# Attention and two MoE layers on one core: the first MoE's tokens in chunks of 512, 256, 256 and 512, the second MoE's w_out converted at its use, and two buffers of transposed probabilities

## The chip, the cores and the metric

The kernel runs on one core of one Trainium2 chip. The metric is device time in microseconds (us) from one launch, and the median of several runs is compared. The engines are named as the profile names them: PE is TensorE (PEld its weight loads), DVE is VectorE, ACT is ScalarE, POOL is GpSimd, and SP is the engine whose queue issues all of this kernel's DMAs.

## The reference

```python
# q, k, v: 2 x 8 heads x 768 x 64; window 128, 4 sink columns
scores = np.where(is_sink | in_window, scale * (q @ k.T), -1e9)
a = softmax(scores)
x = (a @ v).transpose(0, 2, 1, 3).reshape(1536, 512)
...
h = x @ w1_in                                   # 512 -> 2048
g = np.where(h >= 1, h, np.where(h <= -1, 0.0, (h + 1) ** 2 / 4))
x = g @ w1_out                                  # 2048 -> 512
...
h = x @ w2_in
g = h * np.clip(h + 3.0, 0.0, 6.0) / 6.0
out = g @ w2_out
```

The weights are 64-bit floats, q, k and v 32-bit ones.

## The kernel before

**The MoE layers.** Tokens (1536) lie along the free dimension, features along the 128 partitions. Each layer is worked through in chunks of N = 512 tokens, three in each layer: chunks 0, 1 and 2 are the first MoE's, chunks 3, 4 and 5 the second's. A chunk has 16 steps, one for each 128 of the 2048 hidden features. A step is an `h_group` (12 matmuls into one of the two banks of `ps_h`) and, LAG = 2 steps later, the `y_group` of the same features (12 matmuls into the four accumulator banks `ps_y`). Every operand is kept as a high and a low part in float32r (`xh`/`xl`, `wih`/`wil`, `gh`/`gl`, the two halves of `wo`), and every product is three matmuls. Between `h_group` and `y_group`, ACT and DVE apply the activation and split the result into `gh` and `gl`: five operations in the first MoE, four in the second.

**The weights.** A 64-bit weight tile (`raw`, 512 KB, four buffers) is loaded, turned into a float32 tile `w` by ACT, DVE and POOL (`narrow`), and split into a high and a low part: `take`. A tile of w_in stays in SBUF until its layer is over. A tile of w_out is used by one step of each chunk: its two parts are written to HBM (`wo_d`) and read back (`load_wo`) by later chunks. `queue` says at which step each tile is taken. The second MoE's w_out is taken in steps 16 to 31, that is during chunk 1, into tiles of its own called `early`, and its w_in during chunk 2.

**The attention.** The 48 units of work (128 queries of two heads each) stand in four groups: group 0 is done ahead of chunk 0 (the prologue), and the others are spread over the slots of the steps (four slots in a step). While chunk c runs, the attention of chunk c + 1's tokens is done. For a unit PE first computes two scores (`ps_s`, one bank for each head), DVE adds the mask and takes the maximum (L326), ACT exponentiates (L345), DVE normalises (L337 to L340). Three units later PE transposes the probabilities (`turn`: `ps_t`; `sinks`: `ps_k`), ACT copies them out of PSUM into `pt` and `pts` (L364), and one unit after the last transpose of a pair of heads `mix` multiplies them with v (`ps_v`), and the result goes into the next chunk's `xh` and `xl`. There is one `pt` buffer, so that the first copy of the next pair waits for the mix of this pair. Once the first `y_group` has begun, scores, transposes and mixes share two PSUM banks (pool `ps_a`).

**What sets the order.** PE and SP run in the order in which the code is written. The order of DVE, ACT and POOL is laid out ahead by a scheduler with a timeline of its own. [...]

**Outputs of a chunk** are written to HBM (`x2_d`) at the chunk's end and read back as the second MoE's input (`load_x`, at step 4 of the chunk before).

Of the kernel before, what the change touches and what calls it, by code (L numbers as in the profile page):

```python
# [16 lines left out]
P = 128  # L17
# [4 lines left out]
F64_HIGH = 122879.984375  # L22


N = 512

GROUPS = [(0, 0, 0, 4), (1, 0, 4, 2), (1, 1, 0, 2), (2, 1, 2, 4)]

DIST = 3
MIX_LAG = 1  # L30
# [39 lines left out]
def f32(ap):  # L70
    return ap.bitcast(F32)
# [3 lines left out]
def sink_attention_moe_moe_kernel(  # L75
# [20 lines left out]
    FC = w1_in.shape[0]  # L96
    SCALE = 1.0 / float(D) ** 0.5
    fast = fast_case(S, n_sink, window)
    NCH = NT // N
    chunks = [(m, c * N) for m in range(2) for c in range(NCH)]  # L100

    consts = ctx.enter_context(tc.tile_pool(name="consts", bufs=1))
    wpool = ctx.enter_context(tc.tile_pool(name="w", bufs=1))
# [7 lines left out]
    ps_a = ctx.enter_context(tc.tile_pool(name="ps_a", bufs=2, space=bass.MemoryType.PSUM))  # L111


    x2_d = [[dram.tile([DM, N], F32R, name=f"x2{part}{c}_d") for part in "hl"] for c in range(NCH)]
    wo_d = [[dram.tile([P, 2 * DM], F32R, name=f"wo{m}_{fc}_d") for fc in range(FC)] for m in range(2)]


# [33 lines left out]
    xparts = {}  # L151

    def x_tile(ci, part, dtype, name):
        return x_p.tile([P, KC, N], dtype, tag=f"{part}{ci % 2}", name=f"{name}{ci}", bufs=1)
# [41 lines left out]
    def take(m, which, fc):  # L196

        t = raw.pop((m, which, fc))
        if which == "i":
            hi = wpool.tile([P, DM], F32R, tag=f"wih{fc}", name=f"wih{m}_{fc}")  # L200
            lo = wpool.tile([P, DM], F32R, tag=f"wil{fc}", name=f"wil{m}_{fc}")
            wi[m, fc] = (hi.rearrange("p (k f) -> p k f", f=P), lo.rearrange("p (k f) -> p k f", f=P))
        else:
            w = wo_tile(m, fc) if m == 0 else wo_p.tile([P, 2, DM], F32R, tag="early", name="early", bufs=2)
            hi, lo = w[:, 0, :], w[:, 1, :]

        def split(src):
# [38 lines left out]
    def build_fast_attention(at_p):  # L246
# [121 lines left out]
        def turn(j, u):  # L368
            b, i0, nq, first, nb = geom(pairs[j][0])
            i = i0 + u  # L370
            if u == 0:
                pt[j] = (
                    at_p.tile([P, 2, NQ, 2, P], F32, tag="pt", name="pt", bufs=1),
                    at_p.tile([NS, 2, NQ, P], F32, tag="pts", name="pts", bufs=1),
                )
            p = probs[j, u]
            w = widths[min(i, 2)]
            ps = bank("ps_t").rearrange("p (e n q) -> p e n q", e=2, n=2)
            lo = 1 if i == 0 else 0
# [138 lines left out]
    gparts, ytiles = {}, {}  # L518

    def load_x(ci):  # L520
        m, t0 = chunks[ci]
        for part, t in zip((0, 1), x_tiles(ci)):
            nc.sync.dma_start(out=f32(t), in_=f32(x2_d[ci - NCH][part]).rearrange("(k p) n -> p k n", p=P))

    def load_x1(ci):
        xh, xl = x_tiles(ci)
        src = x1_d[0]
        for kc in range(KC):
            t = g_p.tile([P, N], F32, tag="r", name="xraw")
            nc.sync.dma_start(out=t, in_=src[kc * P:(kc + 1) * P, chunks[ci][1]:chunks[ci][1] + N])  # L530
            high(xh[:, kc, :], t, N)
            low(xl[:, kc, :], t, xh[:, kc, :], N)
# [95 lines left out]
    with tc.manual_schedule(engines={mybir.EngineType.PE, mybir.EngineType.SP}):  # L628
        nc.vector.memset(half, 0.5)
        make_identity(nc, ident)  # L630
        with ExitStack() as att:
# [17 lines left out]
            for s in range(len(seq) + LAG):  # L649
# [71 lines left out]
```

## Time and profile before

| | us |
|---|---|
| median of 3 runs | 715.59 (714.6 to 723.47) |
| profiled execution, own time | 720.04 |
| its span, first to last instruction | 718.2 |
| PE busy, share of the span | 670.4, 93% |
| DVE busy | 418.7, 58% |
| ACT busy | 329.2, 46% |
| POOL busy | 98.2, 14% |

The profile was taken from one execution, whose own time is 1.8 us above its span and 4.45 us above the median. The busy shares are means over parts with different limits: the prologue runs from 0 to 69.2 us, chunk 0 to 225.1, chunk 1 to 360.7, and the other four chunks and the last two `y_group`s fill the rest.

### The profile page before, as it was taken

Reading aid. Unit: us, or ns where it says so; the run is one execution under the profiler, and the core shown is the slowest. Engines: PE = TensorE matmul, PEld = TensorE weight load, DVE = VectorE, ACT = ScalarE, POOL = GpSimd, SP = SyncE. Lnnn points to the kernel's source line nnn. Section 1 sums busy time; section 2 is a strip of 40 time slices with the busy share of each in tenths; the row PEclk is TensorE's granted clock in tenths of the full one; section 3 lists DMA queues with packets and bytes.
Section 4 is the critical chain, followed back from the end, with each engine's and each line's share of the span. In section 5 each row is a group of like instructions: output and inputs, shape, how many; then the busy total and the mean of one; then the engine's idle time right before and its main releaser. Section 6 shows DMA issues by size and latency. Waiting matters only on the chain.

```text
span 718.2 us, 8789 instructions
## 1 busy us (share of the span) xinstructions
PE 670.4 (93%) x3008; PEld 506.3 (70%) x3008; DVE 418.7 (58%) x916; ACT 329.2 (46%) x674; POOL 98.2 (14%) x83
## 2 busy tenths in 40 slices
PE   6888778988889999989999999999999999999997
PEld 3445555656557656667688888888888888888886
DVE  5989987779766777678377996322223222232222
ACT  6678856565554656366345563322222222222222
POOL 2212251313102021113001431000000000000000
PEclk9989988799989989999999999999999999999999
DMA  7144636365347668196539842472326432152221
GB/s 264 63 133 140 216 117 201 115 191 188 116 139 253 223 253 309 42 358 204 177 115 381 304 168 88 167 273 88 103 74 212 175 112 88 60 205 89 89 88 59
DMA packets 45869, 119.16 MB, mean 166 GB/s; under 512 B 4304, under 2 KB 13568, under 8 KB 45824
## 3 DMA queue, kind: packets, MB, share of 16 engines
q1 hardware_dynamic: 45824, 118.60, 47.8%
q8 instruction: 24, 0.39, 0.2%
q14 instruction: 21, 0.17, 0.1%
HBM read 92.36 MB, written 26.21 MB: 165 GB/s over the span
## 4 chain that ended last, share of the span: by engine, by line
PE 66%; DVE 16%; DMA 10%; ACT 4%; SPq 2%; issue 2%; POOL 0%; ACTq 0%; POOLq 0%
PE ps_y L586 30%; PE ps_h L542 29%; PE ps_v L419 5%; DMA raw1o<-moe_w_out_dram 3%; DMA raw0o<-moe_w_out_dram 3%; DVE p L340 2%; PE ps_s L319 2%; DMA raw0i<-moe_w_in_dram 2%; DVE w L190 2%; DVE p L326 2%; DVE w L188 2%; ACT w L185 1%; DVE ps_h L553 1%; DVE r L552 1%; DVE wil L149 1%
## 5 line engine op out<-in xcount | busy, mean ns | idle before, releaser
L586 PE MATMUL ps_y<-gh,wo 128*128 128x512 f32 x768 | 263.1, 400 | 1.7 <-DVE xl L149 1.7
L586 PEld LDWEIGHTS ps_y<-gh,wo 128*128 128x128 f32 x768 | 146.3, 190 | 35.9 <-issue 3.9
L542 PE MATMUL ps_h<-xh,wih 128*128 128x512 f32 x384 | 155.7, 405 | 2.1 <-ACT xh L142 1.6
L542 PE MATMUL ps_h<-xl,wih 128*128 128x512 f32 x384 | 151.5, 394 | 0.5 <-DVE xl L149 0.5
L586 PE MATMUL ps_y<-gl,wo 128*128 128x512 f32 x384 | 151.4, 394 | 0.0
L542 PE MATMUL ps_h<-xh,wil 128*128 128x512 f32 x384 | 151.4, 394 | 0.0
L149 DVE TENSOR_TENSOR gl<-ps_h,gh 128x512 fp32r<-128x512 f32 x96 | 66.1, 689 | 102.3 <-ACT gh L142 101.8
L142 ACT ACTIVATE gh<-ps_h 128x512 fp32r<-128x512 f32 x96 | 57.2, 596 | 134.7 <-PE ps_y L586 109.9
L556 DVE SCALAR_TENSOR_TENSOR ps_h<-r,ps_h 128x512 f32<-128x512 f32 x48 | 33.4, 696 | 103.8 <-ACT r L555 103.8
L542 PEld LDWEIGHTS ps_h<-xh,wih 128*128 128x128 f32 x384 | 72.9, 190 | 24.0 <-issue 7.1
L319 PE MATMUL ps_s<-kraw,qraw 64*128 64x260 f32 (+2 forms) x192 | 55.2, 471 | 32.9 <-DVE nm L326 26.1
L542 PEld LDWEIGHTS ps_h<-xh,wil 128*128 128x128 f32 x384 | 73.1, 190 | 15.6
L542 PEld LDWEIGHTS ps_h<-xl,wih 128*128 128x128 f32 x384 | 73.1, 190 | 14.6 <-DVE xl L149 0.8
L586 PEld LDWEIGHTS ps_y<-gl,wo 128*128 128x128 f32 x384 | 73.4, 191 | 13.9
L555 ACT ACTIVATE r<-ps_h,half 128x512 f32<-128x512 f32 x48 | 33.0, 688 | 104.1 <-PE ps_h L542 104.1
L319 PEld LDWEIGHTS ps_s<-kraw,qraw 64*128 64x128 f32 x192 | 26.6, 217 | 56.7 <-DVE nm L326 37.9
L345 ACT ACTIVATE p<-p,nm 128x260 f32<-128x260 f32 (+2 forms) x96 | 46.6, 486 | 33.0 <-DVE nm L326 32.5
L552 DVE SCALAR_TENSOR_TENSOR r<-r 128x512 f32<-128x512 f32 x48 | 39.8, 829 | 17.3 <-ACT r L551 17.3
L326 DVE CUSTOM_DVE_ANT_0 p<-ps_s,mask 128x260 f32<-128x260 f32 (+2 forms) x96 | 36.8, 396 | 13.9 <-PE ps_s L319 13.8
L188 DVE TENSOR_SCALAR w<-w 128x512 f32<-128x512 f32 x64 | 32.4, 506 | 20.8 <-ACT w L185 20.6
L340 DVE TENSOR_SCALAR p<-p,sm 128x260 f32<-128x260 f32 (+2 forms) x96 | 40.2, 458 | 0.7
L551 ACT ACTIVATE r<-ps_h,half 128x512 f32<-128x512 f32 x48 | 32.6, 680 | 16.4 <-PE ps_h L542 16.3
(62 smaller groups left out, 666.5 us busy)
## 6 DMA issues: line engine op xcount, KB each, us to landing
wo<-wo_d SPq DMA_DIRECT2D x80, 512.0 KB, 5.2
raw0i<-moe_w_in_dram SPq DMA_DIRECT2D x16, 512.0 KB, 5.6
raw0o<-moe_w_out_dram SPq DMA_DIRECT2D x16, 512.0 KB, 4.6
wo_d<-wo SPq DMA_DIRECT2D x16, 512.0 KB
raw1o<-moe_w_out_dram SPq DMA_DIRECT2D x16, 512.0 KB, 7.8
wo_d<-early SPq DMA_DIRECT2D x16, 512.0 KB, 4.9
raw1i<-moe_w_in_dram SPq DMA_DIRECT2D x16, 512.0 KB
x2h_d<-yh SPq DMA_DIRECT2D x12, 256.0 KB, 2.3
```

Source lines behind the costliest of these rows:

```text
L142: nc.scalar.activation(out=dst, in_=src, func=AF.Copy)
L149: nc.vector.tensor_tensor(out=dst, in0=src, in1=f32(hi), op=ALU.subtract)
L188: nc.vector.tensor_scalar(out=f32(c), in0=f32(c), scalar1=F64_LOW, scalar2=F64_HIGH, op0=ALU.max, op1=ALU.min)
L319: nc.tensor.matmul(banks[e], tq[rows, u * P:(u + 1) * P], tk[rows, c0:c0 + w], start=True, stop=True)
L326: nc.vector.tensor_tensor_reduce(out=p[:, e, :], in0=banks[e], in1=masks[min(i, 2)], scale=-SCALE, scalar=BIG, op0=ALU.add, op1=ALU.min, a ...
L340: nc.vector.tensor_scalar_mul(out=p[:, e, :], in0=p[:, e, :], scalar1=sm[:, e:e + 1])
L345: nc.scalar.activation(out=p[:, e, :], in_=p[:, e, :], func=AF.Exp, scale=-1.0, bias=nm[:, e:e + 1], accum_out=sm[:, e:e + 1],)
L419: nc.tensor.matmul(ps[e * D:(e + 1) * D, u0 * P:u1 * P], l, r, start=n == 0, stop=n == len(ops[0]) - 1)
L542: nc.tensor.matmul(ps, w[:, kc, :], x[:, kc, :], start=i == 0, stop=i == len(ops) - 1)
L552: nc.vector.scalar_tensor_tensor(out=r, in0=r, scalar=1.0, in1=r, op0=ALU.min, op1=ALU.mult)
L556: nc.vector.scalar_tensor_tensor(out=ps, in0=r, scalar=1.0, in1=ps, op0=ALU.min, op1=ALU.mult)
L586: nc.tensor.matmul(ys[dm], a[:, cs], b, start=fc == 0 and i == 0, stop=fc == FC - 1 and i == 2)
```

## The change

The first MoE has four chunks, of 512, 256, 256 and 512 tokens; the second keeps three of 512. So there are seven chunks, 0 to 3 and 4 to 6. Every tile keeps its size, and the 256-token chunks use half of it: their matmuls have 256 moving columns, and their ACT and DVE operations 256 elements. Group 1 of the attention belongs to chunk 1 and group 2 to chunk 2, so chunk 0 runs beside 8 units of attention instead of 16, chunk 1 beside the next 8, and chunk 2 (256 tokens) beside group 3, as chunk 1 (512 tokens) did before. The converted tiles of w_out are now read back in chunks 1, 2 and 3, and 5 and 6.

The second MoE's w_out is taken in steps 64 to 79, during chunk 4, straight into the tiles that chunk 4's `y_group`s read; the `early` tiles are gone. Its w_in is taken in steps 49 to 64, during chunk 3.

There are two buffers of `pt` and `pts`. The HBM copies of x2 are one tensor for all chunks instead of one for each.

```diff
+CHUNKS = [[512, 256, 256, 512], [512, 512, 512]]
-GROUPS = [(0, 0, 0, 4), (1, 0, 4, 2), (1, 1, 0, 2), (2, 1, 2, 4)]
+GROUPS = [(0, 0, 0, 4), (1, 0, 4, 2), (2, 1, 0, 2), (3, 1, 2, 4)]
...
-    NCH = NT // N
-    chunks = [(m, c * N) for m in range(2) for c in range(NCH)]
+    NCH = len(CHUNKS[0])
+    chunks = [(m, sum(CHUNKS[m][:c]), n) for m in range(2) for c, n in enumerate(CHUNKS[m])]
...
-            w = wo_tile(m, fc) if m == 0 else wo_p.tile([P, 2, DM], F32R, tag="early", name="early", bufs=2)
+            w = wo_tile(m, fc)
...
-                    at_p.tile([P, 2, NQ, 2, P], F32, tag="pt", name="pt", bufs=1),
-                    at_p.tile([NS, 2, NQ, P], F32, tag="pts", name="pts", bufs=1),
+                    at_p.tile([P, 2, NQ, 2, P], F32, tag="pt", name="pt", bufs=2),
+                    at_p.tile([NS, 2, NQ, P], F32, tag="pts", name="pts", bufs=2),
...
-        ps = ps_h.tile([P, N], F32, tag="h", name="ps_h")
+        ps = ps_h.tile([P, N], F32, tag="h", name="ps_h")[:, :n]
...
     for fc in range(FC):
-        queue.append((FC + fc, 1, "o", fc))
-    for fc in range(FC):
+        queue.append((NCH * FC + fc, 1, "o", fc))
         queue.append(((NCH - 1) * FC + 1 + fc, 1, "i", fc))
...
-                if 0 <= a < len(seq) and seq[a][0] not in (0,):
+                if 0 <= a < len(seq) and seq[a][0] not in (0, NCH):
                     load_wo(chunks[seq[a][0]][0], seq[a][1])
```

**PE in chunk 0, where a pair of heads follows another.** The row with ps_s is a unit's two scores, ps_v the mix of the earlier pair, and what stands in brackets is the engines whose semaphores a row waits for. Before, from the second half of a `y_group` to the mix:

```order
L319 MATMUL ps_s<-kraw,qraw 128x128 [waits DMAHW1_49,DMAHW0_49,DVE_49]
L319 MATMUL ps_s<-kraw,qraw 128x128 [waits DVE_49]
L586 MATMUL ps_y<-gh,wo_917 128x512
L586 MATMUL ps_y<-gl,wo_917 128x512
L586 MATMUL ps_y<-gh,wo_917 128x512 x2
L586 MATMUL ps_y<-gl,wo_917 128x512
L586 MATMUL ps_y<-gh,wo_917 128x512
L419 MATMUL ps_v<-pts,vs 64x256 [waits DMAHW6_49,DVE_49]
```

And in the changed kernel at the same unit, three steps later in the chunk (the mix stands half an `h_group` behind the last row):

```order
L321 MATMUL ps_s<-kraw,qraw 128x128 [waits DMAHW6_49,DMAHW5_49,DVE_49]
L321 MATMUL ps_s<-kraw,qraw 128x128 [waits Activation_49]
L589 MATMUL ps_y<-gh,wo_1138 128x512
L589 MATMUL ps_y<-gl,wo_1138 128x512
L589 MATMUL ps_y<-gh,wo_1138 128x512 x2
L589 MATMUL ps_y<-gl,wo_1138 128x512
L589 MATMUL ps_y<-gh,wo_1138 128x512
```

The second score waited for DVE, and waits now for ACT. Of the 27 units scored in chunk 0 and after, 10 had a second score that waits for DVE; in the changed kernel 1 has.

**DVE while group 3 of the attention is done.** `ps_h`, `r` and `gl` are the MoE's activation and split, `p`, `nm` and `sm` the attention, `raw1o`, `w` and `early` the conversion of the second MoE's w_out. Before, a step and a half of chunk 1:

```order
L149 TENSOR_TENSOR early<-w_2563,early 128x512
L149 TENSOR_TENSOR gl<-ps_h,gh 128x512
L188 TENSOR_SCALAR w_2787<-w_2787 128x512
L189 TENSOR_SCALAR raw1o_2548<-raw1o_2548 128x512
L326 ISA p,nm<-ps_s,mask_136 128x260
L326 ISA nm 128x1
L190 SCALAR_TENSOR_TENSOR w_2787<-w_2787,raw1o_2548 128x512
L552 SCALAR_TENSOR_TENSOR r<-r 128x512
L326 ISA p,nm<-ps_s,mask_136 128x260
L326 ISA nm 128x1
L149 TENSOR_TENSOR early<-w_2641,early 128x512
L553 TENSOR_TENSOR ps_h<-ps_h,r 128x512
```

And a step of chunk 2 of the changed kernel:

```order
L150 TENSOR_TENSOR gl<-ps_h,gh 128x256
L555 SCALAR_TENSOR_TENSOR r<-r 128x256
L339 TENSOR_SCALAR sm<-sm 128x2
L556 TENSOR_TENSOR ps_h<-ps_h,r 128x256
L340 RECIPROCAL sm<-sm 128x2
L342 TENSOR_SCALAR p<-p,sm 128x260 x2
L150 TENSOR_TENSOR gl<-ps_h,gh 128x256
L328 ISA p,nm<-ps_s,mask_132 128x260
L328 ISA nm 128x1
L328 ISA p,nm<-ps_s,mask_132 128x260
L328 ISA nm 128x1
```

No conversion stands between them any more, in chunk 1 and chunk 2 alike, and the MoE's rows have half the elements.

**DVE in chunk 4 of the changed kernel**, the second MoE's first, where before only the L556 and `gl` rows and four `yl` of the chunk before stood:

```order
L559 SCALAR_TENSOR_TENSOR ps_h<-r,ps_h 128x512
L190 TENSOR_SCALAR w_4843<-w_4843 128x512
L191 TENSOR_SCALAR raw1o_4694<-raw1o_4694 128x512
L192 SCALAR_TENSOR_TENSOR w_4843<-w_4843,raw1o_4694 128x512
L150 TENSOR_TENSOR gl<-ps_h,gh 128x512
L190 TENSOR_SCALAR w_4888<-w_4888 128x512
L191 TENSOR_SCALAR raw1o_4739<-raw1o_4739 128x512
L192 SCALAR_TENSOR_TENSOR w_4888<-w_4888,raw1o_4739 128x512
L559 SCALAR_TENSOR_TENSOR ps_h<-r,ps_h 128x512
L150 TENSOR_TENSOR wo_4842<-w_4843,wo_4842 128x512
```

The low part of w_out tile 7 is made behind the activation of step 6 of that chunk; the `y_group` that reads it is in step 9.

## Rows read from the trace of the kernel before

**Rows 1.** Busy time by stage: stretch, length, PE, PEld, DVE, ACT, POOL, clock, DMA.

```profile
0.00:69.20 69.20, 55.53 (x241) 30.53 (x241) 56.68 (x203) 49.22 (x136) 16.54 (x29) 0.93 0.46 147
69.20:225.10 155.90, 134.63 (x594) 92.89 (x593) 120.45 (x289) 90.65 (x199) 37.09 (x25) 0.90 0.51 166
225.10:360.70 135.60, 126.45 (x617) 90.16 (x617) 96.08 (x211) 75.58 (x157) 24.68 (x17) 0.97 0.62 225
360.70:447.70 87.00, 87.00 (x385) 72.09 (x384) 71.76 (x107) 45.69 (x77) 19.84 (x13) 1.00 0.60 218
447.70:534.80 87.10, 87.10 (x386) 72.12 (x386) 24.78 (x37) 22.85 (x36) 0.00 (x0) 1.00 0.41 145
```

**Rows 2.** The chain that ended last, in order of time: start, length, what.

```profile
298.81 2.91 PE ps_v L419 x24
...
371.75 2.72 PE ps_h L542 x12
```

**Rows 3.** What PE waited for in chunk 0: total us, times, longest.

```profile
PE ps_s L319 <- DVE nm L326: 14.3, 8, 3.8
```

**Rows 4.** What PE waited for in chunk 1.

```profile
PE ps_s L319 <- DVE nm L326: 2.6, 2, 1.5
```

**Rows 5.** Timeline around one such wait in chunk 0: start, length, engine.

```profile
97.60 0.48 PE L319 MATMUL ps_s<-kraw,qraw 64*128 64x128 f32 x2
...
101.57 0.28 DVE L326 CUSTOM_DVE_ANT_0 p<-ps_s,mask 128x128 f32<-128x128 f32 x1
...
101.91 0.79 PE L319 MATMUL ps_s<-kraw,qraw 64*128 64x128 f32 x2 [3.83 <-DVE nm L326]
```

**Rows 6.** Busy time in the stretch behind that wait, columns as Rows 1.

```profile
100.00:111.00 11.00, 9.09 (x30) 5.87 (x31) 7.67 (x20) 4.02 (x10) 4.52 (x3) 0.53 0.11 24
```

**Rows 7.** Two waits of ACT over the whole span.

```profile
ACT pt L364 <- PE ps_v L419: 19.4, 11, 5.8
...
ACT w L185 <- DMA raw1o<-moe_w_out_dram: 12.3, 6, 4.1
```

**Rows 8.** Busy time in parts of chunk 0, columns as Rows 1.

```profile
69.20:111.00 41.80, 33.47 (x152) 22.46 (x151) 36.55 (x90) 27.70 (x60) 14.27 (x9) 0.88 0.50 163
69.20:153.20 84.00, 70.25 (x313) 47.95 (x311) 70.10 (x164) 52.97 (x113) 25.72 (x17) 0.86 0.51 164
153.20:225.10 71.90, 64.37 (x284) 44.94 (x283) 50.36 (x126) 37.69 (x86) 11.37 (x9) 0.95 0.52 168
```

**Rows 9.** DVE's groups by shape over the whole span.

```profile
L340 DVE TENSOR_SCALAR p<-p,sm 128x260 f32<-128x260 f32 x64 | 26.9, 461 | 0.4
...
L326 DVE CUSTOM_DVE_ANT_0 p<-ps_s,mask 128x260 f32<-128x260 f32 x64 | 25.9, 420 | 5.5 <-PE ps_s L319 5.4
...
L337 DVE TENSOR_SCALAR sm<-sm 128x2 f32<-128x2 f32 x48 | 13.6, 287 | 5.6 <-ACT p L345 5.4
...
L149 DVE TENSOR_TENSOR xl<-ps_v,xh 128x512 fp32r<-128x512 f32 x8 | 5.5, 687 | 9.6 <-ACT xh L142 9.6
...
L149 DVE TENSOR_TENSOR xl<-ps_v,xh 128x256 fp32r<-128x256 f32 x8 | 3.3, 417 | 2.8 <-ACT xh L142 2.8
```

**Rows 10.** PE's timeline in chunk 0, transposes and a score.

```profile
74.67 0.27 PE L382 MATMUL ps_t<-ident,p 128*128 128x128 f32 x1
...
75.46 0.48 PE L542 MATMUL ps_h<-xh,wih 128*128 128x512 f32 x1
...
77.03 0.71 PE L319 MATMUL ps_s<-kraw,qraw 64*128 64x260 f32 x4
77.67 0.50 PE L542 MATMUL ps_h<-xh,wih 128*128 128x512 f32 x1
```

**Rows 11.** Weight loads at the same place.

```profile
75.44 0.19 PEld L542 LDWEIGHTS ps_h<-xh,wih 128*128 128x128 f32 x1
75.55 0.19 PEld L542 LDWEIGHTS ps_h<-xl,wih 128*128 128x128 f32 x1
```

**Rows 12.** Issues of the tiles of w_out that are read back: count, size, us to landing.

```profile
wo<-wo_d SPq DMA_DIRECT2D x80, 512.0 KB, 5.2
```

More of the change, by code (lines that the diff above doesn't have):

```diff
@@ L111, in sink_attention_moe_moe_kernel @@
     ps_a = ctx.enter_context(tc.tile_pool(name="ps_a", bufs=2, space=bass.MemoryType.PSUM))
-    x2_d = [[dram.tile([DM, N], F32R, name=f"x2{part}{c}_d") for part in "hl"] for c in range(NCH)]
+    x2_d = [dram.tile([DM, NT], F32R, name=f"x2{part}_d") for part in "hl"]
     wo_d = [[dram.tile([P, 2 * DM], F32R, name=f"wo{m}_{fc}_d") for fc in range(FC)] for m in range(2)]
@@ L153, in x_tile @@
     def x_tile(ci, part, dtype, name):
-        return x_p.tile([P, KC, N], dtype, tag=f"{part}{ci % 2}", name=f"{name}{ci}", bufs=1)
+        t = x_p.tile([P, KC, N], dtype, tag=f"{part}{ci % 2}", name=f"{name}{ci}", bufs=1)
+        return t[:, :, :chunks[ci][2]]
     def x_tiles(ci):
@@ L520, in load_x @@
     def load_x(ci):
-        m, t0 = chunks[ci]
-        for part, t in zip((0, 1), x_tiles(ci)):
-            nc.sync.dma_start(out=f32(t), in_=f32(x2_d[ci - NCH][part]).rearrange("(k p) n -> p k n", p=P))
+        m, t0, n = chunks[ci]
+        for part, t in zip(x2_d, x_tiles(ci)):
+            nc.sync.dma_start(out=f32(t), in_=f32(part).rearrange("(k p) n -> p k n", p=P)[:, :, t0:t0 + n])
     def load_x1(ci):
@@ L527, in load_x1 @@
         src = x1_d[0]
+        m, t0, n = chunks[ci]
         for kc in range(KC):
[L529 to L532, printed above, removed]
+            t = g_p.tile([P, N], F32, tag="r", name="xraw")[:, :n]
+            nc.sync.dma_start(out=t, in_=src[kc * P:(kc + 1) * P, t0:t0 + n])
+            high(xh[:, kc, :], t, n)
+            low(xl[:, kc, :], t, xh[:, kc, :], n)
     def h_group(s, slot):
         ci, fc = seq[s]
-        m, _ = chunks[ci]
+        m, _, n = chunks[ci]
         hi, lo = wi[m, fc]
         xh, xl = x_tiles(ci)
-        ps = ps_h.tile([P, N], F32, tag="h", name="ps_h")
+        ps = ps_h.tile([P, N], F32, tag="h", name="ps_h")[:, :n]
         ops = [(w, x, kc) for kc in range(KC) for w, x in ((hi, xh), (hi, xl), (lo, xh))]
@@ L544, in h_group @@
                 slot()
-        r = g_p.tile([P, N], F32, tag="r", name="r")
-        gh = g_p.tile([P, N], F32R, tag="gh", name="gh")
-        gl = g_p.tile([P, N], F32R, tag="gl", name="gl")
+        r = g_p.tile([P, N], F32, tag="r", name="r")[:, :n]
+        gh = g_p.tile([P, N], F32R, tag="gh", name="gh")[:, :n]
+        gl = g_p.tile([P, N], F32R, tag="gl", name="gl")[:, :n]
         with tc.high_priority(200):
@@ L556, in h_group @@
                 nc.vector.scalar_tensor_tensor(out=ps, in0=r, scalar=1.0, in1=ps, op0=ALU.min, op1=ALU.mult)
-        bal.tensor(len(ops) * N / 2.26)
-        bal.add("act", 260 + N / 1.2)
-        bal.add("dve", (2 - m) * (150 + N / 0.96))
+        bal.tensor(len(ops) * n / 2.26)
+        bal.add("act", 260 + n / 1.2)
+        bal.add("dve", (2 - m) * (150 + n / 0.96))
         def split():
             with tc.high_priority(200):
-                high(gh, ps, N, True)
-                low(gl, ps, gh, N)
+                high(gh, ps, n, True)
+                low(gl, ps, gh, n)
         defer(split)
@@ L571, in y_group @@
         ci, fc = seq[s]
-        m, t0 = chunks[ci]
+        m, t0, n = chunks[ci]
         w = wo.pop((m, fc))
@@ L577, in y_group @@
             spare.clear()
-            ytiles[ci] = [ps_y.tile([P, N], F32, tag=f"y{i}", name="ps_y") for i in range(KC)]
+            ytiles[ci] = [ps_y.tile([P, N], F32, tag=f"y{i}", name="ps_y")[:, :n] for i in range(KC)]
         ys = ytiles[ci]
@@ L586, in y_group @@
                 nc.tensor.matmul(ys[dm], a[:, cs], b, start=fc == 0 and i == 0, stop=fc == FC - 1 and i == 2)
-            bal.tensor(3 * N / 2.26)
+            bal.tensor(3 * n / 2.26)
             if fc == FC - 1:
@@ L594, in y_group @@
                         nc.vector.tensor_copy(out=t, in_=ys[dm])
-                    nc.sync.dma_start(out=out[cs, t0:t0 + N], in_=t)
+                    nc.sync.dma_start(out=out[cs, t0:t0 + n], in_=t)
                 else:
-                    high(t, ys[dm], N, True)
-                    low(parts[1][:, dm, :], ys[dm], t, N)
+                    high(t, ys[dm], n, True)
+                    low(parts[1][:, dm, :], ys[dm], t, n)
                     for part in range(2):
-                        nc.sync.dma_start(out=f32(x2_d[ci][part])[cs, :], in_=f32(parts[part][:, dm, :]))
+                        nc.sync.dma_start(out=f32(x2_d[part])[cs, t0:t0 + n], in_=f32(parts[part][:, dm, :]))
             if dm == KC // 2 - 1:
```

## The prediction

> **What bounds the kernel now.** I read the busy time by stage first [rows 1]. From 360.7 us on PE is busy in every microsecond at the full clock, and the chain consists of nothing but PE pieces of 2.72 us, 12 matmuls of 512 columns each [rows 2]: 5.44 us for a step, 226.7 ns for a matmul, 87.0 us for a chunk. Only fewer or cheaper matmuls would help there. Ahead of it chunk 0 takes 155.9 us and chunk 1 135.6 us for the same MoE work, 87 us each.
>
> What PE must do there besides is the attention. Its prices: a score unit delays the next matmul by 0.64 us (77.03 to 77.67), eight transposes take 0.79 us (74.67 to 75.46), so 0.1 each [rows 10], and a mix of 24 matmul records 2.91 us, 0.12 each [rows 2]. By the order of the instructions chunk 1 holds 11 scores, 92 transposes and 4 mixes of 24: 7.0 + 9.2 + 11.6 = 28 us, so PE's floor is 87 + 28 = 115 and the overhead 21 us. Chunk 0 holds 16 scores, 72 transposes, 4 mixes of 16 and 4 of 8: 10.2 + 7.2 + 11.5 = 29; its MoE part lacks two y groups (81.6); floor 110.5, overhead 45.
>
> The overhead has three parts. In chunk 0 PE waits 14.3 us in 8 pieces for the row maximum, in chunk 1 2.6 us in 2 [rows 3, 4]. The timeline shows what that is [rows 5]: the first score of a unit ends near 98.1, DVE comes to its maximum only at 101.57, since other work stands ahead of it in its queue, and the second score starts at 101.91. Both scores use one bank: the other is held by a transpose whose copy waits for the earlier pair's mix, for there is one pt buffer. ACT loses 19.4 us to the same thing in 11 pieces, one for each pair after the first [rows 7]. [...] Over chunk 0 the clock is 0.90, over chunk 1 0.97 [rows 1]: 155.9 x 0.10 + 135.6 x 0.03 = 20 us of full-speed time. Third, DVE is close to full where two weight tiles are taken in a step: 87% in the first part of chunk 0 [rows 8].
>
> **The change part by part.**
>
> *Columns.* Chunks 1 and 2 run 2 x 384 = 768 matmuls of 256 columns, where 384 of 512 ran. Half of 226.7 would be 113.4 ns. [...] Lower bound: 0.1 us, the pace of the transposes, each of which loads 128 weight columns too [rows 10]. Upper bound: the 190 ns for which a weight load is recorded, if nothing overlapped it [rows 11]. I take 120, because two loads start 0.11 us apart [rows 11], so that a load fits under 120 ns. The cost is 768 x 6.6 ns = +5 us, and a chunk's MoE floor is 46.1 us.
>
> [...]
>
> *Small fixed costs.* The 32 half steps bring 16 more of each activation and split operation. DVE's takes 687 ns for 512 elements and 417 for 256 [rows 9], so 147 ns are fixed: 3 x 16 x 0.147 = 7 us of DVE, on a queue with room in those chunks (below), so nothing on the path.
>
> *Two pt buffers.* The first copy of a pair no longer waits, the bank comes free, and 10 second scores that waited for DVE become 1. That takes 14.3 + 2.6 us of waits and most of the lower clock behind them. What is late next is DVE's queue itself: the normalised probabilities, and the first score's bank. I don't count the 17 + 20 us as a gain in one sum, but work out each stage anew.
>
> *Chunk 0.* The attention of group 2 leaves it. On DVE a unit costs 2 x (0.42 + 0.46) + 0.29 = 2.05 us and some small operations [rows 9]; I put it at 2.4 with them, 2.1 for the narrow units of group 2, so 8 units with 4 splits (0.42 each) and their share of the rest take about 21 us, an estimate. The 24 weight conversions stay. First half of the chunk: DVE has 70.1 us of work in 84 [rows 8], 59.6 remain; at the best share seen, 87%, that is 68.5 us. Second half: PE's floor is 43.5 + 9 = 52.5, and DVE's work 50.4 - 10.5 = 40 us is below it; before, this half stood 14 us over its floor, nearly all second-score waits and lower clock; I leave 2. So 68.5 + 54.5 = 123 us for 155.9.
>
> *Chunk 1 of the new order* holds 8 scores, 26 transposes and 4 mixes of 8: 5.1 + 2.6 + 3.9 = 12, floor 46 + 12 = 58. No conversion is left on DVE: 16 x 3 x 0.42 = 20 us for the MoE and 19 for the attention. I add 7 us: about half a microsecond for each of 8 units, and 3 where chunk 0's 2 MB of results go out on SP's queue ahead of the next w_out tile. 65 us.
>
> *Chunk 2 of the new order* holds what chunk 1 held, 28 us, floor 46 + 28 = 74. DVE has 20 + 11 x 2.4 + 3 = 49 us, where chunk 1 before had 96.1 [rows 1]: the conversions are gone, and with them ACT's 12.3 us of waits for raw1o [rows 7]. Before, the overhead was 21; without the second scores' 2.6 and the clock's 4 it is 14, which I keep, since a step is only half as long. 88 us.
>
> *The second MoE's w_out at its use.* In chunk 4 it meets DVE with 24.8 us of work in 87; chunk 2 before carried the same 16 conversions (of w_in) beside a dearer activation, 71.8 us, and held PE up nowhere [rows 1]. On SP's queue and the DMA engines 16 raw loads and 16 writes move to chunk 4, and its 16 reads go; that is what the old chunk 2 moved too (loads and reads, 218 GB/s). POOL's 16 additions come along; it has nothing else there. New is that the tile is needed soon. By the order, tile 7's low part is made behind step 6's activation and read in step 9: two steps or more of 5.44 us cover it. If they didn't, a y group would wait for DVE's part, (71.8 - 16 x 3 x 0.69) / 16 = 2.4 us a tile, 39 in all. I take 0. Chunk 3 (w_in) is the old chunk 2.
>
> *Prologue.* Three of its four pairs come after the first, so 3 of the 11 pt waits, 1.8 us each [rows 7], lie there; DVE is busy for 56.7 of 69.2 us [rows 1], so I take 2 us, between 0 and 5.
>
> Sum: (123 + 65 + 88) - (155.9 + 135.6) = -15.5, with the prologue -17.5, and 720.04 - 17.5 = 702.5 for the profiled execution. The median lies 4.45 below that execution: 698.
>
> **The rivals.**
>
> *More is gained.* If PE's waits in chunk 0 were the cause of DVE's idle time and not the other way round, DVE would run at 95% in its first half (63 us) and the second half at 53; chunks 1 and 2 would lose 2 and 6 us: 116 + 60 + 80 = 256, and 680 in all. For it: DVE idles 14 of the first 84 us while PE waits as well [rows 8]. Against: 87% is the highest share seen.
>
> *Nothing is gained.* Group 3's attention now stands beside half the MoE work, with the same two banks: between two attention steps PE has 6 matmuls of 120 ns, 0.7 us, to hide an ACT or DVE operation of 0.4 to 0.6 us and its queue. If each of the 16 units costs 0.9 us more, chunk 2 takes 102: 712. For it: chunk 1's overhead before. Against: DVE's and ACT's queues lose the conversions exactly there. That the buffers do nothing belongs here.
>
> *Slower.* The weight loads set the pace: at 190 ns a matmul [rows 11] the 768 matmuls cost 768 x 70 ns = 54 us more, 752. It decides from 128 ns a load (+6 us) upward, and the kernel turns slower at 143 (+17.5). Against: the loads 0.11 us apart.
>
> *Late w_out tiles.* The tiles for a step are issued at most about two and a half steps ahead, 9 us in a chunk of 3.5 us steps, against a landing of 5.2 [rows 12]. If they took 14 us, steps would be 5.6 us: +25 in chunk 1, 725.
>
> **How the numbers follow.** The forecast has 0.52 and lies between 685 and 708 (chunk 0 at 112 to 130, columns at 113 to 128 ns); more gained 0.17; nothing gained 0.24; the two slow ones 0.07 together. Two per cent, about what can be told from no change, are 701.3 and 729.9. Faster by more than that: all of the second case and seven tenths of the first, 0.54; within: 0.41; slower: 0.05. The range takes in the middle of the second case and all of the third: 677 to 718.
>
> **What would show it.** Chunk 0 near 123 us with PE's waits for the row maximum below 5 us and a clock above 0.95; matmuls of 256 columns 120 ns apart; chunks 1 and 2 at 65 and 88; no PE gap from chunk 3 on. It is wrong if chunk 0 stays above 140 (DVE or DMA hold it), if the columns cost 150 ns or more, or if chunk 4 has gaps before its y groups.

## The result and the profile after

The changed kernel takes 690.91 us (median of 4 runs, 689.69 to 691.18) against 717.04 (4 runs, 714.6 to 723.47; the three runs ahead of the prediction had a median of 715.59). The ratio, of the means of these runs, is 0.9619, its 95% interval 0.9553 to 0.9685. The prediction was 698.0 with a range of 677 to 718, and "faster by over 2%" as the likeliest. The profiled execution has 690.73 us and a span of 688.6.

Busy time by stage, to lay beside [rows 1] (same columns): chunk 0, the new chunks 1 and 2, chunk 4 with the conversions of w_out, and the two halves of chunk 0, which answer to [rows 8].

```profile
68.30:192.50 124.20, 108.94 (x505) 80.18 (x504) 109.75 (x221) 77.24 (x155) 37.65 (x25) 0.95 0.58 187
192.50:254.80 62.30, 61.99 (x475) 55.38 (x474) 37.74 (x123) 30.02 (x81) 1.54 (x1) 1.00 0.63 219
254.80:332.50 77.70, 77.70 (x618) 65.49 (x617) 41.37 (x145) 41.26 (x107) 0.00 (x0) 1.00 0.45 154
418.00:505.20 87.20, 87.20 (x385) 72.15 (x386) 58.82 (x92) 44.18 (x74) 18.52 (x14) 1.00 0.60 223
68.30:132.70 64.40, 53.81 (x247) 38.80 (x245) 60.89 (x121) 44.48 (x89) 22.60 (x15) 0.92 0.65 208
132.70:192.50 59.80, 55.13 (x259) 41.38 (x260) 48.85 (x101) 32.76 (x67) 15.05 (x10) 0.97 0.50 163
```

Chunks 0 to 2 take 264.2 us where chunks 0 and 1 took 291.5: 27.3 of the 29.6 us by which the span falls. The prologue gives 0.9 more and chunk 3 gives 1.5. In chunk 2 PE is busy in every one of the 77.70 us, and chunk 4 bears the conversions at 87.2.

What PE waited for in chunk 0 (us in total, times, longest), to lay beside [rows 3]:

```profile
PE ps_h L545 <- DVE gl L150: 10.3, 4, 5.9
PE ps_v L421 <- DVE nm L328: 2.5, 1, 2.5
PE ps_s L321 <- ACT pt L366: 1.2, 1, 1.2
PE ps_y L589 <- ACT pt L366: 0.6, 1, 0.6
```

The 14.3 us in which second scores waited for the row maximum are gone. Of ACT's two waits of [rows 7] the one for `ps_v` is gone, and the one for `raw1o` is 2.8 us for 12.3, both ACT operations that read the tile counted. A wait that took 0.5 us in chunk 0 before stands in their place: the next `h_group` waits for `gl`, whose subtraction frees the bank. PE's timeline shows the longest of them (start, length, idle time and its end in brackets):

```profile
75.29 0.40 PE L545 MATMUL ps_h<-xh,wil 128*128 128x512 f32 x1
81.54 0.79 PE L545 MATMUL ps_h<-xh,wih 128*128 128x512 f32 x1 [5.85 <-DVE gl L150]
```

The timeline's rows of DVE and POOL, with the one ACT row that makes `gh`, show what DVE does meanwhile. `gh` is there at 78.29, but conversions (`wo`, `w`) and the activation of the next step (`r`) stand ahead of `gl` in DVE's queue, and POOL adds beside it:

```profile
77.24 0.41 DVE L190 TENSOR_SCALAR w<-w 128x512 f32<-128x512 f32 x1
77.54 1.58 POOL L196 TENSOR_TENSOR w<-w,raw0i 128x512 int32<-128x512 int32 x1 [2.05 <-DVE w L192]
77.57 0.42 DVE L191 TENSOR_SCALAR raw0o<-raw0o 128x512 int32<-128x512 int32 x1
77.72 0.57 ACT L143 ACTIVATE gh<-ps_h 128x512 fp32r<-128x512 f32 x1
77.91 1.77 DVE L150 TENSOR_TENSOR wo<-w,wo 128x512 fp32r<-128x512 f32 x1
79.60 0.68 DVE L192 SCALAR_TENSOR_TENSOR w<-w,raw0o 128x512 int32<-128x512 int32 x1
80.20 0.68 DVE L555 SCALAR_TENSOR_TENSOR r<-r 128x512 f32<-128x512 f32 x1
80.51 1.52 POOL L196 TENSOR_TENSOR w<-w,raw0o 128x512 int32<-128x512 int32 x1 [1.38 <-ACT w L187]
80.81 0.68 DVE L150 TENSOR_TENSOR gl<-ps_h,gh 128x512 fp32r<-128x512 f32 x1
```

In chunk 1 a matmul of 256 columns starts every 0.12 us, `h_group` and `y_group` alike (PE's timeline):

```profile
251.93 0.28 PE L545 MATMUL ps_h<-xh,wih 128*128 128x256 f32 x1
252.05 0.28 PE L545 MATMUL ps_h<-xl,wih 128*128 128x256 f32 x1
252.17 0.28 PE L545 MATMUL ps_h<-xh,wil 128*128 128x256 f32 x1
```

### The profile page after: what moved, and what is told of

Same layout as the page of the kernel before. It is cut to its first block, busy times and chain, and to the rows that moved or that the text cites. A ratio compares the mean times of both kernels' runs of the same rounds, so it can differ in the third digit from the quotient of the medians.

```text
span 688.6 us, 9625 instructions
## 1 busy us (share of the span) xinstructions
PE 656.1 (95%) x3392; PEld 522.8 (76%) x3392; DVE 429.2 (62%) x968; ACT 337.0 (49%) x710; POOL 97.7 (14%) x83
## 4 chain that ended last, share of the span: by engine, by line
PE 78%; DVE 12%; DMA 6%; ACT 2%; SPq 1%; issue 1%; POOL 0%; ACTq 0%; DVEq 0%; POOLq 0%
PE ps_y L589 34%; PE ps_h L545 34%; PE ps_v L421 5%; PE ps_s L321 3%; DVE w L192 2%; DMA raw0i<-moe_w_in_dram 2%; DVE w L190 2%; DMA raw0o<-moe_w_out_dram 1%; DVE p L328 1%; DVE wo L150 1%; PE ps_t L385 1%; PE ps_t L384 1%; DMA wo<-wo_d 1%; DVE wil L150 1%; DVE raw0i L191 1%; DVE p L342 1%
## 5 line engine op out<-in xcount | busy, mean ns | idle before, releaser
L589 PE MATMUL ps_y<-gh,wo 128*128 128x512 f32 (+1 forms) x896 | 268.8, 364 | 0.9 <-ACT pt L366 0.6
L545 PE MATMUL ps_h<-xh,wih 128*128 128x512 f32 (+1 forms) x448 | 166.6, 372 | 11.0 <-DVE gl L150 11.0
L545 PE MATMUL ps_h<-xl,wih 128*128 128x512 f32 (+1 forms) x448 | 162.1, 362 | 0.4 <-DVE xl L150 0.4
L545 PE MATMUL ps_h<-xh,wil 128*128 128x512 f32 (+1 forms) x448 | 161.9, 361 | 0.0
L589 PE MATMUL ps_y<-gl,wo 128*128 128x512 f32 (+1 forms) x448 | 161.2, 360 | 0.0
L150 DVE TENSOR_TENSOR gl<-ps_h,gh 128x512 fp32r<-128x512 f32 (+1 forms) x112 | 68.6, 613 | 91.4 <-ACT gh L143 90.9
L143 ACT ACTIVATE gh<-ps_h 128x512 fp32r<-128x512 f32 (+1 forms) x112 | 60.0, 536 | 130.3 <-PE ps_y L589 91.8
L558 ACT ACTIVATE r<-ps_h,half 128x512 f32<-128x512 f32 x48 | 33.0, 688 | 87.5 <-PE ps_h L545 87.5
L555 DVE SCALAR_TENSOR_TENSOR r<-r 128x512 f32<-128x512 f32 (+1 forms) x64 | 47.7, 745 | 14.9 <-ACT r L554 14.7
L190 DVE TENSOR_SCALAR w<-w 128x512 f32<-128x512 f32 x64 | 40.1, 626 | 13.4 <-ACT w L187 13.3
L554 ACT ACTIVATE r<-ps_h,half 128x512 f32<-128x512 f32 (+1 forms) x64 | 36.6, 571 | 15.9 <-PE ps_h L545 15.5
```

The source lines that it names most:

```text
L190: nc.vector.tensor_scalar(out=f32(c), in0=f32(c), scalar1=F64_LOW, scalar2=F64_HIGH, op0=ALU.max, op1=ALU.min)
```

## The experiments

Two theories stood at the start. **Serial scores**: one pt buffer holds a PSUM bank, the second scores wait, the clock falls behind the wait (0.53 in [rows 6]); two buffers are the change that counts. **Crowded DVE**: the conversions and the number of attention units in DVE's queue are the cause, so that the moves of work (group 2 out of chunk 0, w_out out of chunk 1) count. The ten runs took the three parts apart. Stages are in us, from one profiled execution of each kernel; each ratio is to the kernel before on the same chip.

| kernel | chunk 0 | 1, or 1 and 2 | median | ratio (95%) |
|---|---|---|---|---|
| before | 155.9 | 135.6 | 717.04 | 1 |
| e1: w_out at its use | 161.5 | 122.3 | 710.49 | 0.9902 (0.9861 to 0.9943) |
| e4: smaller pools | 146.8 | 129.0 | 708.47 | 0.9889 (0.9795 to 0.9983) |
| e3: smaller pools, two pt | 132.3 | 128.1 | 687.47 | 0.9555 (0.9477 to 0.9633) |
| e9: one pt, mix earlier | 136.9 | 134.6 | 698.93 | 0.9707 (0.9631 to 0.9784) |
| e2: w_out at its use, two pt | 130.6 | 119.8 | 678.72 | 0.9452 (0.9391 to 0.9513) |
| after: the same and 256-token chunks | 124.2 | 140.0 | 690.91 | 0.9619 (0.9553 to 0.9685) |
| e10: two pt, 256, smaller pools, w_out early | 119.3 | 174.4 | 720.64 | 1.0028 (0.9996 to 1.0061) |
| e5: e2, 256 in the second MoE | 129.5 | 119.9 | 683.89 | 0.9493 (0.9444 to 0.9542) |
| e6: after, w_in spread | 117.8 | 140.0 | 685.21 | 0.9512 (0.9467 to 0.9557) |
| e7: e2, w_in spread | 131.6 | 119.8 | 684.48 | 0.9492 (0.9432 to 0.9552) |
| e8: e7, attention later | 141.2 | 119.9 | 688.64 | 0.9593 (0.9514 to 0.9673) |

**e1: w_out at its use, alone.**

```diff
-            w = wo_tile(m, fc) if m == 0 else wo_p.tile([P, 2, DM], F32R, tag="early", name="early", bufs=2)
+            w = wo_tile(m, fc)
...
-        queue.append((FC + fc, 1, "o", fc))
-    for fc in range(FC):
+        queue.append((NCH * FC + fc, 1, "o", fc))
...
-                if 0 <= a < len(seq) and seq[a][0] not in (0,):
+                if 0 <= a < len(seq) and seq[a][0] not in (0, NCH):
```

> The kernel before with one part of the change: the second MoE's w_out is converted in its own first chunk (chunk 3 here), straight into the tiles of use. Chunks of 512, one pt buffer. Serial-scores theory (the one pt buffer holds a bank, second scores wait for DVE, and the lower clock follows): chunk 0 stays at 156 +- 4 us with some 14 us of second-score waits, chunk 1 loses a part of its 21 us of overhead only, 128 to 133; 708 to 713 for the median. Crowded-DVE theory (the conversions and the number of attention units in DVE's queue are the cause, the buffer is not): chunk 1 falls to 115 to 122 once the 16 conversions have left it, chunk 0 stays; 698 to 705. Both: chunk 3, which now holds the conversions, stays within 2 us of 87.

Measured: 710.49. Busy time by stage (chunks 0 and 1):

```profile
68.90:230.40 161.50, 138.78 (x594) 95.78 (x593) 122.30 (x293) 92.00 (x203) 38.04 (x25) 0.87 0.50 158
230.40:352.70 122.30, 121.24 (x617) 88.69 (x616) 58.64 (x149) 51.41 (x110) 1.54 (x1) 1.00 0.32 111
```

Chunk 1 goes from 135.6 to 122.3 with DVE's work from 96 to 59 us: there the crowded-DVE theory holds, within 0.3 us of its range. Chunk 0 keeps its waits and even takes 5.6 us more, so that the median is in the other theory's range (708 to 713). Of PE's waits in chunk 0:

```profile
PE ps_s L319 <- DVE nm L326: 14.2, 7, 3.8
```

**e2: the whole change but for the 256-token chunks** (e1's edits and two buffers of `pt` and `pts`).

> The kernel before with w_out converted at its use and two buffers of pt and pts: the whole change but for the chunks of 256. Serial-scores theory: second-score waits for DVE in chunk 0 fall from 14.3 us to below 4 and the clock there rises from 0.90 to 0.95 or more, chunk 0 takes 130 to 140 us for 155.9, chunk 1 115 to 122; 680 to 692, and the chunks of 256 columns give nothing. Crowded-DVE theory: chunk 0 still holds 120 us of DVE work with 16 units, and stays at 148 to 156 with the wait renamed (PE waits for gl or for the probabilities); chunk 1 115 to 122; 695 to 705, and the chunks of 256 give the rest down to 691.

Measured: 678.72, below both ranges, and faster than the changed kernel; the two intervals don't meet. Busy time (chunk 0, chunk 1, first half of chunk 0):

```profile
67.70:198.30 130.60, 121.40 (x595) 85.72 (x594) 117.92 (x287) 89.02 (x201) 37.96 (x25) 0.97 0.62 198
198.30:318.10 119.80, 119.80 (x617) 88.09 (x616) 58.72 (x149) 51.75 (x110) 1.53 (x1) 1.00 0.33 113
67.70:136.60 68.90, 62.47 (x313) 43.37 (x311) 67.28 (x159) 52.53 (x116) 24.05 (x16) 0.95 0.63 199
```

All 16 units and all 24 conversions are still in chunk 0, with 117.9 us of DVE work for 120.5, and yet it is 25.3 us shorter. PE's idle time there falls from 155.9 - 134.6 = 21.3 to 9.2 us; the lower clock, estimated from the granted shares 0.97 and 0.90, takes 130.6 x 0.03 = 4 where it took 155.9 x 0.10 = 16. DVE works for 67.3 of 68.9 us in the first half: full, but it was no limit at the old length. Serial scores it is, in chunk 0.

**e3 and e4: two buffers alone, and its base.** The space for the second `pt` comes from other tiles. Both runs have one `early` for two and two `w32` for three, and e3 has the two buffers of `pt` and `pts` besides.

```diff
-            w = wo_tile(m, fc) if m == 0 else wo_p.tile([P, 2, DM], F32R, tag="early", name="early", bufs=2)
+            w = wo_tile(m, fc) if m == 0 else wo_p.tile([P, 2, DM], F32R, tag="early", name="early", bufs=1)
...
-            t32 = raw_p.tile([P, DM], F32, tag="w32", name="w32", bufs=3)
+            t32 = raw_p.tile([P, DM], F32, tag="w32", name="w32", bufs=2)
```

> The kernel before with two buffers of pt and pts alone. The space for them comes from one early tile less (1 for 2) and one w32 tile less (2 for 3); the kernel with only these two cuts runs beside it. Serial-scores theory: against that kernel 12 to 25 us less, chunk 0 at 130 to 142, second-score waits below 4 us. Crowded-DVE theory: less than 5 us less, chunk 0 above 148. If the missing tiles hold up DVE, both kernels are slower than the kernel before, in chunk 1 above all.

> The kernel before with one early tile for two and two w32 tiles for three, nothing else: the base for the run with two pt buffers alone. All theories: between no change and 10 us slower than the kernel before, the loss in chunk 1, where early is used; chunk 0 within 3 us of 155.9.

Measured: 687.47 and 708.47, 21.0 us apart. Chunk 0 of e4 and of e3:

```profile
70.10:216.90 146.80, 128.51 (x595) 89.48 (x593) 122.20 (x285) 91.19 (x199) 34.58 (x25) 0.95 0.54 174
68.40:200.70 132.30, 118.75 (x595) 83.80 (x594) 114.91 (x288) 88.87 (x200) 38.07 (x25) 1.00 0.62 196
```

The second buffer takes 14.5 us off chunk 0 (the two profiled executions differ by 17.0 us in all). The second scores' waits for the row maximum there go from this line of e4 to none in e3, and the granted clock of chunk 0 is 1.00 for 0.95:

```profile
PE ps_s L319 <- DVE nm L326: 11.4, 7, 3.6
```

That the base is itself faster than the kernel before (interval 0.9795 to 0.9983) was not expected: its chunk 0 came out 9 us shorter. The likely reason is that smaller pools give DVE, ACT and POOL another order; no run shows it apart. So a difference of 9 us in chunk 0 between two of these kernels need not come from what was changed there.

**e9: the bank freed in another way**, with one buffer.

```diff
-MIX_LAG = 1
+MIX_LAG = 0
```

> The kernel before, with one pt buffer and everything else as it was, but each mix one unit earlier (MIX_LAG 0 for 1). The earlier pair's mix then stands ahead of the next pair's transposes on PE, so that no copy holds a bank for it; by the order of the instructions no more second scores wait for DVE than with two buffers. Serial-scores theory: the second-score waits in chunk 0 fall from 14.3 us to below 4 without any more space, and chunk 0 comes from 155.9 to 130 to 142 us, less what the mix itself now waits for its last copy (8 mixes of about half a microsecond to one in chunk 0): 690 to 703 for the median. Rival, that two buffers gave more room to ACT and DVE and the banks do not matter: no change, 710 to 722, or slower, since PE waits for every mix's copy.

Measured: 698.93; chunk 0 at 136.9, in the range of the first theory, with no wait for the row maximum of a second score left among PE's waits there:

```profile
69.10:206.00 136.90, 122.83 (x594) 85.85 (x593) 115.64 (x284) 87.85 (x200) 36.95 (x24) 0.96 0.56 188
```

Its chunk 1, which keeps the conversions, stays at 134.6. So it is the held bank that counts, not the space: with the bank freed chunk 0 loses 19.0 us here, 14.5 from e4 to e3 and 30.9 from e1 to e2, all more than the 9 us above.

**e10: the 256-token chunks with w_out still early.** The changed kernel with e1's edits undone and the smaller pools of e4.

> The changed kernel with the second MoE's w_out converted early again, in chunk 1 (now one of 256 columns), into one early tile, and with two w32 tiles for three: chunks and two pt buffers without the third part. Chunks 1 and 2 took 62.3 and 77.7 us with no conversion in them. If the conversions only matter where DVE is full, 16 of them (some 38 us of DVE work on top of 37.7 in a chunk of 62) fill chunk 1: 75 to 85 us, chunk 2 at 78, and 700 to 710 for the median. If PE alone sets these chunks, they stay within 3 us and the median is 687 to 694, as with w_out at its use. Chunk 0 stays at 120 to 126 by both.

Measured: 720.64, no gain at all. Chunks 1 and 2, and what PE waited for in them:

```profile
187.00:270.90 83.90, 69.20 (x475) 60.50 (x474) 62.72 (x171) 51.70 (x119) 16.06 (x12) 0.93 0.88 311
270.90:361.40 90.50, 81.40 (x619) 68.30 (x618) 46.92 (x157) 46.32 (x116) 5.18 (x4) 0.95 0.53 181
```

```profile
PE ps_y L589 <- DMA wo<-wo_d: 23.8, 14, 6.5
```

Chunk 1 is in the range that I named for a full DVE, but chunk 2 and the median are above theirs, and the reason was another: DVE is at 75%, and PE waits for the tiles of w_out that are read back. These 23.8 us are all of PE's idle time in the two chunks. In chunk 1 the DMA engines are busy for 88% at 311 GB/s, with these transfers among them (issues, size, us to landing):

```profile
wo_d<-early SPq DMA_DIRECT2D x13, 512.0 KB, 3.0
wo<-wo_d SPq DMA_DIRECT2D x13, 512.0 KB, 5.4
raw1o<-moe_w_out_dram SPq DMA_DIRECT2D x11, 512.0 KB, 6.5
```

A chunk of half the tokens reads as many weights in half the time, but full DMA engines are not what the trace shows as the cause. In chunks 1 and 2 of the changed kernel, where PE waits 0.3 us for `wo<-wo_d` and chunk 1 has 63% and 219 GB/s, a read-back takes nearly as long to land (4.8 us for 5.4):

```profile
wo<-wo_d SPq DMA_DIRECT2D x32, 512.0 KB, 4.8
```

What differs is when it is issued. In e10 most read-backs stand in SP's queue right behind the write of an `early` tile, and that write waits until DVE has made the tile's low part. This is the largest of SP's waits at these writes (L213) in chunks 1 and 2, and below it the timeline of PE's longest wait:

```profile
SPq L213 <- DVE early L150: 23.6, 6, 5.7
```

```profile
286.22 0.72 DVE L150 TENSOR_TENSOR early<-w,early 128x512 fp32r<-128x512 f32 x1
...
286.97 0.32 SPq L213 DMA_DIRECT2D wo_d<-early  x1
287.34 1.25 SPq L227 DMA_DIRECT2D wo<-wo_d  x2
...
292.52 0.58 PE L589 MATMUL ps_y<-gh,wo 128*128 128x256 f32 x1 [6.53 <-DMA wo<-wo_d]
```

So the conversions do hold up chunks 1 and 2, but by way of SP's queue and not of DVE's time. How much of it is the single `early` tile, which can be filled again only after its write, isn't separated: the same kernel with two wasn't run.

**e5: 256 columns where no attention stands** (the changed kernel with e2's first MoE).

```diff
-CHUNKS = [[512, 256, 256, 512], [512, 512, 512]]
+CHUNKS = [[512, 512, 512], [512, 512, 256, 256]]
...
-GROUPS = [(0, 0, 0, 4), (1, 0, 4, 2), (2, 1, 0, 2), (3, 1, 2, 4)]
+GROUPS = [(0, 0, 0, 4), (1, 0, 4, 2), (1, 1, 0, 2), (2, 1, 2, 4)]
```

> The changed kernel with the first MoE back in three chunks of 512 and the attention groups as they were before, so that only w_out at its use and the two buffers are left of the change (as in the run e2_wt, 678.7 us), and the second MoE in chunks of 512, 512, 256, 256. It puts 768 matmuls of 256 columns where no attention stands. If the 256 columns cost what their rows show (120.0 ns for half of 226.7), it is 5 us over e2_wt: 684. If a chunk of 256 costs more than that by itself (w_out tiles that land late in steps of 2.9 us, the outputs of one more chunk), 688 to 692, and that alone explains why the changed kernel is 12 us over e2_wt; then PE shows gaps in the last two chunks. If the columns cost nothing, 679.

Measured: 683.89, 5.2 us over e2 and 5.3 by the spans (682.0 and 676.7), where 768 x 6.7 ns come to 5.1. The two ran on different chips and their intervals overlap, so the size rests on the trace: no gap in the last two chunks, PE is busy throughout. e5 also has the one x2 tensor in HBM, which e2 lacks; beside the columns that leaves about nothing for it.

```profile
580.50:675.30 94.80, 94.80 (x770) 93.80 (x769) 42.55 (x99) 17.53 (x37) 0.00 (x0) 1.00 0.57 195
```

**e6, e7 and e8: DVE's load in chunk 0 spread**, on the changed kernel (e6) and on e2 (e7); e8 shifts attention to the second half of chunk 0 as well.

```diff
-        queue.append((fc - AHEAD, 0, "i", fc))
+        queue.append((fc - AHEAD if fc < AHEAD else (fc - AHEAD) * 12 // 7, 0, "i", fc))
```

> The changed kernel, with the eight w_in tiles that are taken in steps 0 to 7 of chunk 0 taken in steps 0, 1, 3, 5, 6, 8, 10 and 12 instead. If conversions that stand ahead of gl in DVE's queue hold up chunk 0 (PE waits 10.3 us for gl there, DVE 95% busy in its first half), the waits for gl fall below 5 us and the chunk from 124 to 112 to 118 us: 679 to 686 for the median. If the order of the queue and not its load is the cause, chunk 0 stays within 3 us of 124 and the median within 4 of 691.

> The run e2_wt (512-token chunks, w_out at its use, two pt buffers; 678.7 us) with the w_in tiles of chunk 0 taken in steps 0, 1, 3, 5, 6, 8, 10 and 12. There DVE was busy for 67.3 of the first 68.9 us of chunk 0 and 50.7 of the next 61.7. If DVE's load in the first half is what is left, about 6 us of DVE work move to a half that has 11 us of room: chunk 0 goes from 130.6 to 123 to 127, the median to 671 to 676. If PE's floor or the waits for single results set it, no change: 676 to 681.

> The run before it, and the attention in chunk 0 shifted as well: the first 32 of its 58 slots hold 24 slots' worth of it and the rest the other 34. About 2 of 16 units, 5 us of DVE work, move to the second half. DVE's load theory: chunk 0 at 118 to 124, the median 667 to 674, if the second half does not become the full one (50.7 + 6 + 5 = 62 us of DVE work for a floor of 58 to 60 us of PE). If the second half becomes the bound, the same as the run before or up to 4 us more.

Measured: e6 685.21, chunk 0 at 117.8 and the waits for `gl` at 6.9 us for 10.3, not below 5; the load holds for a part, but the first wait of 5.3 us stays, since DVE's order at that place is the same. Chunk 0 of e6:

```profile
68.80:186.60 117.80, 105.76 (x505) 78.50 (x504) 109.13 (x221) 76.48 (x156) 38.43 (x25) 0.97 0.60 199
```

```profile
PE ps_h L545 <- DVE gl L150: 6.9, 2, 5.3
```

e7 684.48 with chunk 0 at 131.6, no gain: DVE falls from 98% to 88% in the first half and nothing follows. e8 is not faster than e7 (intervals overlap), and its chunk 0, at 141.2, is outside both of its ranges, with a wait of 5.2 us for `gl` like that of the changed kernel and 6.2 us in which scores wait for ACT's copies of `pt` or for DVE. The load theory fails in e2's chunk 0. Chunk 0 of e7 (columns as before):

```profile
68.30:199.90 131.60, 122.66 (x594) 86.04 (x593) 114.34 (x287) 88.27 (x200) 39.58 (x25) 0.97 0.61 195
68.30:136.80 68.50, 62.97 (x313) 43.63 (x311) 60.28 (x149) 47.85 (x107) 20.60 (x14) 0.95 0.58 182
```

## Why the prediction was right, and where it was not

The time fell in the range, and faster by over 2% came true; the gain was larger than the sum had it. Step by step:

**Second scores: right, and underrated.** The waits (14.3 us) and most of the lower clock (by the estimate above 16 us before, 6 after) left chunk 0, as written. But I did not count them as a gain, and put chunk 0's shortening down to group 2's work leaving DVE. (ACT's 11 waits aren't one for each pair after the first, as I read [rows 7]: there are 16 pairs.) e2 shows that 25.3 of the 31.7 us come without moving a unit, e3 and e9 that the bank is the cause.

**Chunk 0, 123 us forecast, 124.2 measured: right sum, wrong limit.** "At the best share seen, 87%" took DVE's idle time in [rows 8] for its capacity. It was idle because PE and the banks waited: without that it ran at 95% (and at 98% in e2). My halves of 68.5 and 54.5 came out at 64.4 and 59.8, so one was 4.1 us too long and the other 5.3 too short; that the sum is near is luck. The new waits for `gl` were not foreseen. Nor did DVE's work fall by the 21 us that I took off: it fell by 10.7, to 60.89 and 48.85 us where I had 59.6 and 40. The operations that stay became longer in the mean, `narrow`'s first one on DVE (L188 before, L190 after) from this line of chunk 0 before to 646 ns; the last section has a reason.

```profile
L188 DVE TENSOR_SCALAR w<-w 128x512 f32<-128x512 f32 x24 | 10.3, 429 | 7.5 <-ACT w L185 7.3
```

The rival "more is gained" had the mechanism: PE's waits were the cause of DVE's idle time.

**Chunk 2, 88 us forecast, 77.7 measured: the mis-sized term.** I kept 14 us of overhead from chunk 1 before. Without conversions it is not there: e1's chunk 1 lost 13.3 us when they left, with one pt buffer. And my floor was low: e2's chunk 1 has PE busy for all of its 119.80 us, so the attention there is 119.8 - 87.0 = 32.8 us of PE and not 28. With 32 the floor of chunk 2 is 78, and the overhead is nothing. Chunk 1 (65 against 62.3) is near by two errors: PE is busy for 61.99 us of it, not 58, two `y_group`s of 512 columns from chunk 0 included, and the 7 us that I added are 0.3.

**Columns: right.** The 120 ns for 256 columns in the sum, 6.6 over half of 226.7, were an estimate of mine: no run of the kernel before shows them, and none shows what the 6.6 consist of. What the runs showed in their place is the pace itself: starts 0.12 us apart in chunk 1 of the changed kernel, where each matmul has its own weight load (474 loads recorded for 475 matmuls), and 5.2 us more in e5 than in e2 for 768 such matmuls.

**w_out at its use: the cost of nothing was right, the worth missed.** It is worth 7 us alone (e1), 9 on top of two pt buffers (e3 to e2), and 30 with the 256-token chunks (e10 to the changed kernel; the smaller pools are in the last two differences). The rival "late w_out tiles" names what happened in e10, though not why: the tiles took 5.4 us to land, not the 14 that it asks for, but were issued late, behind writes that waited for DVE. In the changed kernel, with w_out's conversion moved away, it does not occur.

**What the 256-token chunks do** is the other way round from my sum: they cost. From e2 to the changed kernel the span grows by 688.6 - 676.7 = 11.9 us: 5.1 for the columns; PE's idle time in chunks 0 to 2 from 9.2 to 15.3 + 0.3 us, 6.4 more; the lower clock, by the estimate above, from 3.9 to 6.2, 2.3 more; that is 13.8, two too many for figures that are rounded and stages that overlap. With the w_in tiles spread the spans differ by 683.0 - 677.9 = 5.1 (e6 and e7; the medians by 0.7, since e7's profiled execution is the fastest of its four), no more than the columns. So what goes beyond the columns seems to hang on where conversions and `gl` stand in DVE's order in chunk 0. What of that is the chunks' doing and what the chance of one order isn't settled: chunk 0 is 117.8 to 124.2 in the three kernels with 8 units, 129.5 to 141.2 in the four with 16, two buffers and w_out at its use. The chunks with one pt buffer weren't tried.

**The sum.** 702.5 was forecast for the profiled execution, 690.73 came: 10.3 of the difference from chunk 2, 2.7 from chunk 1, and 1.5 since chunk 3 begins with two `y_group`s of 256 columns (85.5 us for 87); chunk 0 and the prologue give 2.3 back. The 4.45 us that I then took off for the median were luck of another kind: they were how far one execution of the kernel before lay above its median, and the changed kernel's profiled execution lies 0.18 below its own. They made a miss of 12 us into one of 7. Of the signs, PE's waits for the row maximum and the columns came as written; the clock of chunk 0 is 0.95, and chunk 3 has a gap of 0.7 us of PE where I named none. e2, at 678.72, is the version that beats both.

## What to carry to other kernels

An engine's busy share in a stage with waits is not its capacity (DVE's 87% in [rows 8] against 95% in the first half of the changed kernel's chunk 0): before taking the highest share seen as a limit, ask whether it idles because others wait. A change of several parts can have its gain in one and a loss in another, so price each alone: here a second small buffer gave more than all the rest, and halving the chunk took some of it back. When a wait is due to a bank held for a consumer, an earlier consumer (e9) can do much of what a second buffer does (19.0 us off chunk 0 here). And when an engine waits for a transfer, look at what stood ahead of it in its queue before blaming the traffic: in e10 the loads landed about as fast as in the changed kernel (5.4 us for 4.8) and were issued late.

## What the runs showed of the hardware

In chunk 0 of the changed kernel many DVE operations whose operands all lie in SBUF took longer when they started while a POOL addition ran (four `wo` subtractions 1.18 to 1.77 us for 0.68); those with an operand in PSUM did not (the six operations of L556 that start so 0.68 to 0.70 us, the other nine 0.69 to 0.70). In the timeline above, the subtraction for `wo` starts at 77.91, 0.37 us after POOL's addition, and takes 1.77 us; it ends 0.56 after POOL does. The subtraction for `gl`, of the same size but with one operand from PSUM, takes 0.68 beside POOL's next addition (80.51 to 82.03). Over chunk 0 of the changed kernel, DVE's groups by shape (count, busy us, mean ns, idle before):

```profile
L190 DVE TENSOR_SCALAR w<-w 128x512 f32<-128x512 f32 x25 | 16.2, 646 | 8.9 <-ACT w L187 8.9
L150 DVE TENSOR_TENSOR wo<-w,wo 128x512 fp32r<-128x512 f32 x15 | 13.6, 907 | 0.0
L150 DVE TENSOR_TENSOR gl<-ps_h,gh 128x512 fp32r<-128x512 f32 x15 | 10.2, 683 | 2.4 <-ACT gh L143 2.4
```

Of the 15 `wo` subtractions the four that start while POOL adds take 1.18 to 1.77 us, the other eleven 0.68; the four `gl` that start so take 0.68 as well. Operations with one SBUF operand took longer too: nine of L190 start while POOL adds, and take 1.05 us in the mean for 0.42 in the others.

What makes them longer the trace doesn't show; it shows when they start and how long they take, 907 ns in the mean for `wo` against 683 for `gl`. DVE's busy share holds this added time: an L190 that POOL doesn't run ahead of takes 0.41 us (at 77.24), so 25 x (646 - 410) and 15 x (907 - 683) are 9 of the 109.75 us, an estimate for these two groups alone.
